# Mixture of experts in split fp32r: new order tables, a second matrix fetched in parts, and splits on GpSimd in two units

## The chip, the cores and the metric

The kernel runs on one core of a Trainium2 chip. The metric is the device time of one execution in microseconds (us). Engine names in the profile: PE is TensorE, PEld its weight loads, DVE is VectorE, ACT is ScalarE, POOL is GpSimd, SP is SyncE, which here only issues DMAs. A difference under about 0.5% is not told from none by a measurement of this kernel.

## The reference

```python
x = attention(...)                      # (2176, 512): windowed and 32 global tokens
h = np.maximum(x @ w_in, 0.0);  x = h * h @ w_out            # 512 -> 2048 -> 512
P = np.exp(x @ w_gate - max)            # 8 experts
for _ in range(8):                      # Sinkhorn
    P /= P.sum(1, keepdims=True) + 1e-09
    P /= P.sum(0, keepdims=True) + 1e-09
    P *= N / E
for e in range(E):                      # the second mixture, 512 -> 1024 -> 512
    out += P[:, e:e + 1] * (np.maximum(x @ w1[e], 0.0) @ w2[e])
```

Everything is fp32. The change concerns the last loop alone, which fills the program from about 584 us to its end.

## The kernel before, in words

Each fp32 operand is split into a high and a low fp32r part (hi = a cast by ScalarE, lo = operand minus hi, by VectorE or GpSimd), and a product is three matmuls: hi x hi, hi x lo, lo x hi. The second mixture goes over the 2176 tokens in three blocks of 5, 6 and 6 tiles of 128 (`TBS`). A *unit* is one block with one half of an expert's 1024 hidden columns; each block has 16 units (`NS`, `UE` = 2 for an expert). Each matrix product is done by a scheme with seven products in place of eight, on sums of quarter blocks: of the tokens (S1 to S4), of the first matrix and of the second (T1 to T4).

**Block 1** (`first_block`). For every unit s it runs `second_weights(s)` along with the hidden products (`second_hidden`, 14 of them, with a hook after each in which one more step of the other work is issued), then `second_out`, five output tiles of 12 matmuls (line 1121), each read out of PSUM by ScalarE's copy (line 1127, the first half of an expert) or VectorE's addition (line 1131). The output tiles rotate through three PSUM buffers, which the sums of the Sinkhorn iteration (line 851) use too, as that runs beside units 0 and 1. During the output tiles `first_weights(s + 1)` forms the next unit's first matrix: four sums by GpSimd (lines 980 to 986) into the tile `tw`, casts of them by ScalarE (line 997), lo parts by VectorE (line 1000); all forms are written to DRAM (`forms_kept`, line 1032) for blocks 2 and 3. `second_weights(s)` holds four GpSimd sums of the raw second matrix (lines 1010 to 1013), also into `tw`, and one DMA of 1 MB that keeps them in DRAM (`sums_kept`, line 1014); and, for four pieces of the raw matrix, hi by ScalarE (line 1019) and lo by VectorE (line 1021).

**Blocks 2 and 3**: 32 units, here numbered u = 0 to 31. Nothing is transformed again; forms and sums come back from DRAM. All engine work of a unit is listed in a table of `time:operation:arguments` (`USUAL`; `BEFORE_BLOCK` for u = 15, `AFTER_BLOCK` for u = 16); `plan` shifts each table to its unit's start and the operations of all units are issued in the order of these times. Only the order counts: an operation then starts when its engine reaches it and its semaphores allow it. The operations:
- `H:k`, k = 0 to 13: a hidden product, 6 matmuls of 128x384 (line 1373), 84 in a unit; `snap`, `add`, `relu` (lines 1378, 1382, 1386) read it out of PSUM.
- `sum`, `hi`, `lo` (lines 1346, 1333, 1337): the sums S1 to S4 of the hidden layer and the splits of all its quarters, in two halves each; `v` is VectorE, `g` GpSimd.
- `M:i:t`: output product i for tile t, 6 matmuls of 128x256 (line 1403), 126 in a unit, in the order of products 1, 2, 5, 6, 7, 4, 3. Product 5 needs S1, 6 needs S2, 7 needs S3, 4 needs A22, 3 needs S4. `out` gathers one into the accumulator, weighted by the gate (VectorE, line 1419).
- `whi:i`, `wlo:e:i` (lines 1307, 1311): the split of the second matrix for product i, by ScalarE, and by VectorE or GpSimd.
- A piece of the first matrix (256 KB, line 1272) is asked for by SP after each `H:k`, ten pieces ahead, in a ring of ten buffers: what is asked for after `H:0` to `H:3` is used by `H:10` to `H:13`.
- `sums` (line 1291) asks for the next unit's T1 to T4 (1 MB, into `tw`); `rows` (line 1284) for the raw rows of B11, B21 and B22 (two DMAs, 512 and 256 KB).

SP's DMAs are issued in order, and each waits also for the DMA eight before it, since eight semaphores go round.

Of the kernel before, what the change touches and what calls it, by code (L numbers as in the profile page):

```python
# [1596 lines left out]
```

## Time and profile before

| | us |
|---|---|
| median of 3 runs | 2036.81 |
| lowest and highest | 2036.24, 2044.15 |
| profiled execution, its own time | 2037.15 |
| its span, first to last instruction | 2035.3 |
| block 1, unit 0 begins | 584.06 |
| block 2, u = 0 begins (its `H:0`) | 1015.39 |
| u = 15 begins | 1485.71 |
| u = 16 begins | 1518.83 |
| u = 18 begins | 1587.64 |
| last unit, u = 31, begins | 1996.93 |

| engine | busy us, share of the span |
|---|---|
| PE | 1958.3 (96%) |
| DVE | 1500.4 (74%) |
| ACT | 1055.0 (52%) |
| POOL | 805.5 (40%) |

A row of the timeline is the start and length of an instruction (or of several alike in a row, x4), its engine, its line, the operation, output and input, and in brackets the idle time before it and what ended that. Busy time by stretch sums each engine's instructions in a piece of the span; PEclk is the granted TensorE clock as a share of the full one. The wait table sums an engine's idle time by the instruction that ended it.

### The profile page before, as it was taken

How to read it: one execution, taken by the hardware profiler on the slowest of the kernel's cores; microseconds unless marked ns; L12 is line 12 of the kernel's file. 1: busy time of each engine (PE TensorE's matmuls, PEld its weight loads, DVE VectorE, ACT ScalarE, POOL GpSimd, SP SyncE). 2: the span in 40 equal slices, each digit the busy share in tenths (PEclk: the TensorE clock that was granted, in tenths of full speed). 3: DMA queues.
4: the chain of work that ended last, by engine and by line, in shares of the span. 5: the costliest groups of instructions: out<-in, count | busy, mean ns of one | idle time of the engine just before them, and what ended most of it. 6: DMA issues, size and time to landing. Idle time of an engine off the chain costs nothing.

```text
span 2035.3 us, 34904 instructions
## 1 busy us (share of the span) xinstructions
PE 1958.3 (96%) x12482; PEld 1838.7 (90%) x12482; DVE 1500.4 (74%) x3013; ACT 1055.0 (52%) x2357; POOL 805.5 (40%) x815
## 2 busy tenths in 40 slices
PE   8998999999999999999999999999998999999998
PEld 6887798999888899999999999999988999999998
DVE  7999656666467877777777867778687786876867
ACT  7997442333244444444565555555555555555553
POOL 6546332223133455555333433434333342433433
PEclk8999999999999999999999999999999999999999
DMA  7675111112027777777764463553645445354461
GB/s 159 144 145 130 43 63 42 42 63 68 1 89 260 260 265 262 253 263 264 260 219 157 170 215 137 192 187 141 217 155 202 154 173 208 136 200 163 164 215 55
DMA packets 293229, 332.58 MB, mean 163 GB/s; under 512 B 106048, under 2 KB 210496, under 8 KB 286912
## 3 DMA queue, kind: packets, MB, share of 16 engines
q1 hardware_dynamic: 293056, 330.35, 49.5%
q8 instruction: 99, 1.62, 0.3%
q14 instruction: 74, 0.61, 0.1%
HBM read 239.88 MB, written 79.95 MB: 157 GB/s over the span
## 4 chain that ended last, share of the span: by engine, by line
PE 63%; DVE 16%; DMA 11%; ACT 7%; issue 1%; POOL 1%; SPq 1%; DVEq 0%; ACTq 0%; POOLq 0%
PE y L1121 11%; PE oy L1403 10%; DMA w<-forms_kept 10%; PE y L894 9%; PE h L254 9%; PE pa L1373 6%; PE pa L1058 5%; DVE xl L1337 3%; PE pm L1373 3%; DVE hf L1337 3%; DVE acc L1419 3%; DVE hs L1346 3%; PE pd L1058 2%; PE om L1403 2%; PE pb L1373 2%; ACT e L502 2%
## 5 line engine op out<-in xcount | busy, mean ns | idle before, releaser
L1373 PE MATMUL pa<-xh,w 128*128 128x384 f32 x1024 | 293.2, 337 | 16.6 <-DMA w<-forms_kept 15.0
L1373 PEld LDWEIGHTS pa<-xh,w 128*128 128x128 f32 x1024 | 187.8, 188 | 25.4 <-DVE xl L1337 19.1
L1337 POOL TENSOR_TENSOR xl<-acc,xh 128x384 fp32r<-128x384 f32 x64 | 65.4, 1021 | 356.6 <-ACT xh L1333 354.7
L1121 PE MATMUL y<-w,xh 128*128 128x512 f32 x640 | 200.0, 394 | 3.1 <-DVE w L1021 3.1
L894 PE MATMUL y<-hid,w 128*128 128x384 f32 (+1 forms) x960 | 191.1, 357 | 1.3 <-ACT rs L260 1.3
L894 PEld LDWEIGHTS y<-hid,w 128*128 128x128 f32 x960 | 171.8, 188 | 16.6 <-ACT rs L260 1.7
L254 PE MATMUL h<-xh,w 128*128 128x384 f32 (+1 forms) x640 | 181.9, 357 | 1.2 <-ACT rs L260 1.2
L1403 PE MATMUL oy<-w,hf 128*128 128x256 f32 x1152 | 151.6, 286 | 20.8 <-DVE hf L1337 16.6
L1373 PE MATMUL pa<-xl,w 128*128 128x384 f32 x512 | 171.3, 335 | 0.0
L1403 PEld LDWEIGHTS oy<-w,hf 128*128 128x128 f32 x1152 | 142.1, 191 | 27.4 <-DVE hf L1337 22.7
L1419 DVE SCALAR_TENSOR_TENSOR acc<-oy,prob,acc 128x256 f32<-128x256 f32 x366 | 163.6, 472 | 0.7 <-PE oy L1403 0.4
L1307 ACT CAST w<-tw 128x512 fp32r<-128x512 f32 x128 | 79.4, 620 | 162.2 <-PE oy L1403 140.1
L1346 POOL TENSOR_TENSOR hs<-acc 128x384 f32<-128x384 f32 x64 | 85.7, 1358 | 184.6 <-ACT acc L1386 184.6
L1373 PE MATMUL pm<-xh,w 128*128 128x384 f32 x512 | 150.4, 334 | 0.0
L1121 PEld LDWEIGHTS y<-w,xh 128*128 128x128 f32 x640 | 120.7, 190 | 27.9 <-DVE w L1021 3.5
L1403 PE MATMUL oy<-w,xh 128*128 128x256 f32 x768 | 140.7, 283 | 0.0
L260 ACT ACTIVATE r<-h 128x384 f32<-128x384 f32 (+1 forms) x76 | 40.4, 531 | 177.4 <-PE h L254 176.2
L1058 PE MATMUL pa<-xh,w 128*128 128x320 f32 x512 | 129.9, 311 | 0.9 <-DVE z L1074 0.9
L254 PEld LDWEIGHTS h<-xh,w 128*128 128x128 f32 x640 | 117.7, 188 | 14.3 <-ACT r L260 2.7
L115 POOL TENSOR_TENSOR cv<-cv,w 128x512 f32<-128x512 f32 x32 | 48.2, 1515 | 206.5 <-ACT w L113 131.7
L1382 DVE TENSOR_TENSOR acc<-pb,snaps 128x384 f32<-128x384 f32 x64 | 35.7, 557 | 127.3 <-PE pb L1373 124.7
L1121 PE MATMUL y<-w,xl 128*128 128x512 f32 x320 | 125.5, 392 | 0.0
(260 smaller groups left out, 5769.8 us busy)
## 6 DMA issues: line engine op xcount, KB each, us to landing
w<-forms_kept SPq DMA_DIRECT2D x448, 256.0 KB, 5.4
raw<-in_moe_w_dram SPq DMA_DIRECT2D x96, 512.0 KB, 4.9
forms_kept<-w SPq DMA_DIRECT2D x64, 512.0 KB, 6.3
tw<-sums_kept SPq DMA_DIRECT2D x32, 1024.0 KB, 7.5
forms_kept<-w SPq DMA_DIRECT2D x64, 384.0 KB, 6.0
sums_kept<-tw SPq DMA_DIRECT2D x16, 1024.0 KB, 7.6
raw<-in_moe_w_in_dram SPq DMA_DIRECT2D x16, 512.0 KB, 4.2
...
```

Of the source, the lines that this page charges most:

```text
L115: nc.gpsimd.tensor_tensor(out=top, in0=top, in1=f32(hi), op=ALU.subtract)
L254: nc.tensor.matmul(ps, lhsT=w, rhs=x, start=(k == 0), stop=(k == 3 * NC - 1))
L502: nc.scalar.activation(out=v, in_=v, func=AF.Exp, bias=st[:, c : c + 1], scale=-1.0, accum_out=st[:, 4 + c : 5 + c])
L894: nc.tensor.matmul(ps, lhsT=w, rhs=m, start=(f == 0 and x == 0), stop=(f == last and x == 2))
L1058: nc.tensor.matmul(ps, lhsT=lhs, rhs=rhs, start=(first and t == 0), stop=(t == 5), skip_group_check=True)
L1121: nc.tensor.matmul(ps, lhsT=lhs, rhs=rhs, start=(t == 0), stop=(t == 3 * UF - 1))
L1307: nc.scalar.copy(halves_of(out_form[i][0]), source_of(u, i))
L1337: engine.tensor_tensor(out=lo, in0=raws[name][:, q], in1=f32(hi), op=ALU.subtract)
L1346: engine.tensor_tensor(out=raws[name][:, q], in0=raws[a][:, q], in1=raws[b][:, q], op=op)
L1373: nc.tensor.matmul(ps, lhsT=lhs, rhs=rhs, start=(i in (1, 5, 2) and t == 0), stop=(t == 5), skip_group_check=True)
L1403: nc.tensor.matmul(ps, lhsT=lhs, rhs=rhs, start=(i in (5, 1, 2) and y == 0), stop=(y == 5), skip_group_check=True)
L1419: nc.vector.scalar_tensor_tensor(out=acc_, in0=ps, scalar=pr, in1=acc_, op0=ALU.mult, op1=ALU.add)
```

## The change

1. All tables of blocks 2 and 3 are new, and there is one more, `FIRST`, for u = 0. Each has a length of 29.71, where `AFTER_BLOCK` had 30.79.
2. `rows` and `sums` are gone. `raw:i` (`request_raw`) asks for the second matrix of one product, 256 KB, for the next unit; seven of these stand in each table, each behind the last reader of that buffer. The buffers are fixed.
3. In units 0 and 1 of block 1 (`gating`), GpSimd makes the four lo parts of the second matrix, and the four sums with their DMA (`keep_sums`) come after the fourth. In unit 0 the conversion starts with the first hook; before, four hooks went by first.

The lines of the changed kernel shift: 1010 to 1013 become 1012 to 1015, 1014 becomes 1017, 1019 becomes 1026, 1021 becomes 1029, 1127 becomes 1137, 1311 becomes 1313, 1337 becomes 1339, 1346 becomes 1348, 1419 becomes 1421.

```diff
-        add = nc.gpsimd.tensor_tensor
-        add(out=t1, in0=b12, in1=b11, op=ALU.subtract)
...
-        nc.sync.dma_start(out=sums_kept[s].rearrange("p i q d -> p (i q d)"), in_=t.rearrange("p i q d -> p (i q d)"))
+        def keep_sums():
+            add = nc.gpsimd.tensor_tensor
+            add(out=t1, in0=b12, in1=b11, op=ALU.subtract)
...
+            nc.sync.dma_start(out=sums_kept[s].rearrange("p i q d -> p (i q d)"), in_=t_)
+        gating = s < UE
+        if not gating:
+            keep_sums()
         yield
         for f in range(UF):
...
             nc.scalar.copy(hi, r[k][:, q])
             yield
-            nc.vector.tensor_tensor(out=lo, in0=r[k][:, q], in1=f32(hi), op=ALU.subtract)
+            engine = nc.gpsimd if gating else nc.vector
+            engine.tensor_tensor(out=lo, in0=r[k][:, q], in1=f32(hi), op=ALU.subtract)
             yield
             if f == UF - 1:
+                if gating:
+                    keep_sums()
                 for k in range(2):
                     load_pair_of_pieces(s + 1, k, 1)
...
             conv = second_weights(s)
-            wait = 4 if s == 0 else 0
-            hooks = itertools.count()
-            if not wait:
-                next(conv)
+            next(conv)
...
-                if next(hooks) >= wait:
-                    next(conv, None)
+                next(conv, None)
...
-    def request_rows(u):
-    def request_sums(u):
...
+    def request_raw(u, i):
         if u >= LAST:
             return
+        name = OUT_WEIGHT[i]
+        if name in SUMS_AT:
+            src = sums_kept[u % NS][:, SUMS_AT[name]]
+        else:
+            src = second_rows(u % NS, int(name[1]) - 1)[:, :, (int(name[2]) - 1) * DM // 2 :][:, :, 0 : DM // 2]
+        nc.sync.dma_start(out=raw_of(i), in_=src)
...
     USUAL = """
-        1.40:wlo:v:5 2.00:wlo:v:2 2.08:H:2 2.12:sums 2.23:snap:5:0 2.72:rows 3.13:H:3 3.28:add:A11:0
+        4.69:whi:3 4.95:wlo:v:6 5.07:raw:4 5.21:H:5 5.36:snap:5:1 5.55:wlo:v:3 5.73:whi:7 6.25:relu:A11:0
...
-    LENGTH = {USUAL: 29.71, BEFORE_BLOCK: 29.71, AFTER_BLOCK: 30.79}
+    LENGTH = {FIRST: 29.71, USUAL: 29.71, BEFORE_BLOCK: 29.71, AFTER_BLOCK: 29.71}
```

**VectorE in the output products of a usual unit.** `acc` with `hs` out of it is a quarter or a sum S of the hidden layer; `xl` and `hf` are lo parts (`hf` those of S2 and S3); `oy`, `ob`, `om`, `oa` are output products, gathered into `acc`. Before:

```order
L1337 TENSOR_TENSOR xl<-acc,xh 128x384
L1346 TENSOR_TENSOR hs<-acc 128x384
L1337 TENSOR_TENSOR xl<-hs,xh 128x384
L1419 SCALAR_TENSOR_TENSOR acc<-oy,prob,acc 128x256 x2
L1337 TENSOR_TENSOR xl<-hs,xh 128x384
L1346 TENSOR_TENSOR hs<-hs,acc 128x384 x2
L1419 SCALAR_TENSOR_TENSOR acc<-oy,prob,acc 128x256
L1419 SCALAR_TENSOR_TENSOR acc<-ob,prob,acc 128x256
L1337 TENSOR_TENSOR hf<-hs,hf 128x384 x4
L1419 SCALAR_TENSOR_TENSOR acc<-om,prob,acc 128x256
```

Now:

```order
L1339 TENSOR_TENSOR xl<-acc,xh 128x384
L1339 TENSOR_TENSOR xl<-hs,xh 128x384
L1348 TENSOR_TENSOR hs<-acc 128x384 x3
L1348 TENSOR_TENSOR hs<-hs,acc 128x384 x2
L1339 TENSOR_TENSOR xl<-hs,xh 128x384 x2
L1421 SCALAR_TENSOR_TENSOR acc<-oy,prob,acc 128x256 x2
L1421 SCALAR_TENSOR_TENSOR acc<-ob,prob,acc 128x256
L1348 TENSOR_TENSOR hs<-acc 128x384
L1339 TENSOR_TENSOR hf<-hs,hf 128x384 x2
L1421 SCALAR_TENSOR_TENSOR acc<-oy,prob,acc 128x256
L1421 SCALAR_TENSOR_TENSOR acc<-om,prob,acc 128x256
```

Five sums now stand together ahead of the first gathers, where splits and sums alternated before; VectorE makes two of the four lo parts of S2 and S3 instead of all four, and the other two have gone to GpSimd.

**GpSimd in the same unit.** Before:

```order
L1337 TENSOR_TENSOR xl<-acc,xh 128x384 x2
L1346 TENSOR_TENSOR hs<-acc 128x384 x2
L1346 TENSOR_TENSOR hs<-hs 128x384 x2
L1337 TENSOR_TENSOR xl<-hs,xh 128x384 x2
L1311 TENSOR_TENSOR w_71<-tw,w_71 128x512
L1311 TENSOR_TENSOR w_3120<-raw,w_3120 128x512
```

Now:

```order
L1339 TENSOR_TENSOR xl<-acc,xh 128x384 x2
L1339 TENSOR_TENSOR xl<-hs,xh 128x384
L1339 TENSOR_TENSOR hf<-hs,hf 128x384 x2
L1339 TENSOR_TENSOR xl<-acc,xh 128x384
L1348 TENSOR_TENSOR hs<-hs 128x384 x2
```

GpSimd no longer sums out of `acc` in this stretch; it splits instead, and its sums (S4, the last one used) are the only two left. The splits of the second matrix (line 1311) are gone from it.

**SP's queue in a usual unit.** `w` of `forms_kept` is a piece of the first matrix. Before, 1.75 MB stand in a row:

```order
L1272 DMA w_3564<-forms_kept 128x512
L1291 DMA tw<-sums_kept 128x2048
L1284 DMA raw<-in_moe_w_dram 128x2x512
L1284 DMA raw<-in_moe_w_dram 128x2x256
L1272 DMA w_3564<-forms_kept 128x512
L1272 DMA w_3565<-forms_kept 128x512 x2
L1272 DMA w_3566<-forms_kept 128x512 x2
```

Now:

```order
L1279 DMA w_3566<-forms_kept 128x512 x2
L1279 DMA w_3567<-forms_kept 128x512
L1300 DMA tw<-sums_kept 128x512
L1279 DMA w_3567<-forms_kept 128x512
L1279 DMA w_70<-forms_kept 128x512
L1300 DMA raw<-in_moe_w_dram 128x2x256
L1300 DMA tw<-sums_kept 128x512
L1279 DMA w_70<-forms_kept 128x512
L1279 DMA w_3564<-forms_kept 128x512
L1300 DMA tw<-sums_kept 128x512
L1279 DMA w_3564<-forms_kept 128x512
```

The requests for the second matrix now stand singly between the pieces, and further back.

**GpSimd in unit 0 of block 1.** Before:

```order
L986 TENSOR_TENSOR tw<-raw 128x256
L1010 TENSOR_TENSOR tw<-raw 128x512
L1011 TENSOR_TENSOR tw<-raw 128x512
L1012 TENSOR_TENSOR tw<-raw,tw 128x512
L1013 TENSOR_TENSOR tw<-raw,tw 128x512
L980 TENSOR_TENSOR tw<-raw 128x256
L982 TENSOR_TENSOR tw<-raw,tw 128x256
```

Now:

```order
L986 TENSOR_TENSOR tw<-raw 128x256
L1029 TENSOR_TENSOR w_71<-raw,w_71 128x512
L1029 TENSOR_TENSOR w_3394<-raw,w_3394 128x512
L1029 TENSOR_TENSOR w_3343<-raw,w_3121 128x512
L1029 TENSOR_TENSOR w_3343<-raw,w_3343 128x512
L1012 TENSOR_TENSOR tw<-raw 128x512
L1013 TENSOR_TENSOR tw<-raw 128x512
L1014 TENSOR_TENSOR tw<-raw,tw 128x512
L1015 TENSOR_TENSOR tw<-raw,tw 128x512
L980 TENSOR_TENSOR tw<-raw 128x256
L982 TENSOR_TENSOR tw<-raw,tw 128x256
```

The four splits stand ahead of the four sums, and the next unit's sums of line 980 behind both, as before.

## Rows read from the trace of the kernel before

**Rows 1.** Busy time by stretch, from unit start to unit start: us, each engine's busy time, PEclk
```profile
1015.39:1485.71 470.32, 454.98 (x3152) 445.55 (x3150) 354.94 (x692) 259.23 (x526) 178.44 (x152) 1.00 0.51 177
...
1518.83:1556.24 37.41, 31.99 (x212) 31.10 (x211) 31.28 (x58) 19.15 (x38) 11.36 (x10) 0.95 0.52 169
...
1996.93:2035.34 38.41, 30.66 (x212) 29.69 (x210) 24.73 (x46) 13.91 (x29) 9.45 (x8) 0.98 0.22 69
...
1587.64:1618.48 30.84, 30.30 (x213) 29.72 (x212) 23.55 (x47) 17.28 (x35) 11.81 (x10) 1.00 0.50 180
```

**Rows 2.** Chain of waits: start and length of a piece in us, what
```profile
664.71 13.62 PE y L1121 x60
...
1037.70 6.46 PE oy L1403 x52
...
1528.42 2.08 PE pa L1373 x12
```

**Rows 3.** Waits of TensorE, 1015.39 to the end: us in total, times, longest
```profile
PE oy L1403 <- DVE hf L1337: 16.6, 30, 1.3
PE pa L1373 <- DMA w<-forms_kept: 15.0, 22, 1.8
PE oy L1403 <- ACT hf L1333: 3.8, 1, 3.8
```

**Rows 4.** Timeline of VectorE, unit 18: start, us, instruction [idle before <-releaser]
```profile
1603.62 1.37 DVE L1337 TENSOR_TENSOR xl<-hs,xh 128x384 fp32r<-128x384 f32 x1
...
1605.70 0.58 DVE L1337 TENSOR_TENSOR xl<-hs,xh 128x384 fp32r<-128x384 f32 x1
...
1608.13 2.78 DVE L1337 TENSOR_TENSOR hf<-hs,hf 128x384 fp32r<-128x384 f32 x4
1610.83 0.47 DVE L1419 SCALAR_TENSOR_TENSOR acc<-om,prob,acc 128x256 f32<-128x256 f32 x1
```

**Rows 5.** Timeline of GpSimd, unit 18, same columns
```profile
1603.19 2.69 POOL L1346 TENSOR_TENSOR hs<-acc 128x384 f32<-128x384 f32 x2 [5.23 <-ACT acc L1386]
1606.91 2.18 POOL L1346 TENSOR_TENSOR hs<-hs 128x384 f32<-128x384 f32 x2 [1.03 <-DVE hs L1346]
1610.40 2.36 POOL L1337 TENSOR_TENSOR xl<-hs,xh 128x384 fp32r<-128x384 f32 x2 [1.31 <-ACT xh L1333]
...
1614.19 1.29 POOL L1311 TENSOR_TENSOR w<-raw,w 128x512 fp32r<-128x512 f32 x1
```

**Rows 6.** Timeline of SP's DMA queue, unit 18: start, us of issuing, DMA
```profile
1591.45 0.32 SPq L1291 DMA_DIRECT2D tw<-sums_kept  x1
```

**Rows 7.** Busy time by stretch, unit 18; the last three: PEclk, DMA share, GB/s
```profile
1592.00:1604.00 12.00, 12.00 (x74) 11.76 (x73) 6.05 (x12) 8.81 (x20) 2.84 (x3) 1.00 1.01 373
```

**Rows 8.** Busy time by stretch, units 0, 1 and a steady unit of block 1
```profile
584.06:620.16 36.10, 31.92 (x165) 26.31 (x164) 28.57 (x61) 15.88 (x34) 22.29 (x19) 0.95 0.64 211
620.16:650.66 30.50, 28.97 (x153) 25.78 (x152) 26.27 (x66) 12.06 (x27) 11.86 (x12) 0.94 0.64 217
...
678.17:704.11 25.94, 25.94 (x145) 23.58 (x144) 20.35 (x33) 11.48 (x26) 14.61 (x14) 1.00 0.77 261
```

**Rows 9.** Timeline of TensorE, unit 0 of block 1
```profile
606.80 0.50 PE L1121 MATMUL y<-w,xh 128*128 128x512 f32 x1 [3.12 <-DVE w L1021]
```

**Rows 10.** Busy time by stretch, unit 0 of block 1, after that wait
```profile
607.00:611.00 4.00, 4.00 (x11) 3.13 (x11) 4.00 (x6) 1.62 (x3) 3.22 (x5) 0.57 0.45 143
```

**Rows 11.** Timeline of GpSimd, unit 0 of block 1: sums, and line 980 behind them
```profile
587.78 1.73 POOL L1010 TENSOR_TENSOR tw<-raw 128x512 f32<-128x512 f32 x1
...
593.48 1.30 POOL L1013 TENSOR_TENSOR tw<-raw,tw 128x512 f32<-128x512 f32 x1
602.77 0.74 POOL L980 TENSOR_TENSOR tw<-raw 128x256 f32<-128x256 f32 x1 [7.98 <-DMA sums_kept<-tw]
```

**Rows 12.** Timeline of ScalarE, unit 0 of block 1
```profile
606.23 0.62 ACT L997 CAST w<-tw 128x512 fp32r<-128x512 f32 x1 [2.15 <-POOL tw L986]
607.68 0.59 ACT L1127 COPY acc<-y 128x512 f32<-128x512 f32 x1 [0.83 <-PE y L1121]
```

More of the change, by code (lines that the diff above doesn't have):

```diff
@@ L1229, in first_block @@
             else:
-                request_rows(0)
+                rawb.extend(stage.tile([P, 2, 512], F32, tag="r1", name="raw") for _ in range(2))
+                for i in OUT_ORDER:
+                    request_raw(0, i)
                 first_requests()
-                request_sums(0)
                 todo.append(form_splits(1))
@@ L1488 @@
-        32.59:tlo:v:S3 32.70:thi:S2 33.57:tlo:v:S2 34.91:tsum:v:S4 35.89:thi:S4 36.98:tlo:v:S4 37.85:out:4:1
-        38.71:out:4:2
+        -9.27:whi:2 -6.33:whi:6 -5.81:whi:5 -5.29:whi:1 -2.01:whi:4 -1.49:whi:7 -0.90:wlo:v:4 -0.30:wlo:g:7
+        0.00:H:0 0.15:whi:3 1.00:wlo:v:2 1.04:H:1 1.19:snap:1:0 1.60:wlo:g:3 1.72:raw:2 2.08:H:2 2.52:raw:7
+        3.13:H:3 3.28:add:A11:0 3.32:raw:4 3.75:wlo:v:5 4.17:H:4 4.32:thi:A11 4.35:wlo:v:6 4.47:raw:5
+        4.95:wlo:v:1 5.05:relu:A11:0 5.21:H:5 5.27:raw:6 5.47:snap:5:0 5.84:snap:5:1 5.94:tlo:v:A11
@@ new lines @@
+        6.07:raw:3 6.21:snap:1:1 6.25:H:6 6.58:hi:A11:0 6.87:raw:1 7.12:lo:g:A11:0 7.29:H:7 7.44:add:A11:1
+        7.44:thi:A12 8.17:snap:6:0 8.34:H:8 8.54:relu:A11:1 8.68:add:A12:0 9.15:tlo:v:A12 9.38:H:9
+        9.53:snap:6:1 9.90:relu:A12:0 10.32:hi:A11:1 10.42:H:10 10.57:add:A22:0 10.73:hi:A12:0
+        10.86:lo:g:A11:1 11.16:relu:A22:0 11.46:H:11 11.61:add:A12:1 11.86:lo:g:A12:0 12.20:relu:A12:1
+        12.50:H:12 12.65:add:A22:1 12.76:hi:A12:1 13.30:lo:v:A12:1 13.55:H:13 13.70:relu:A21:0
@@ L1490 @@
+        27.70:tsum:v:S3 28.27:M:3:1 28.57:tlo:v:S1 28.68:thi:S3 28.99:M:3:2 29.44:out:3:0 29.44:tsum:g:S2
+        29.83:out:4:0 30.22:out:3:2 30.61:out:3:1 31.00:out:2:1 31.39:tsum:v:S4 31.79:thi:S2 32.52:thi:S4
+        33.45:tlo:v:S2 34.32:tlo:v:S3 35.19:tlo:v:S4 37.73:out:4:1 44.24:out:4:2
     """
     AFTER_BLOCK = """
[L1492 to L1493 removed]
@@ L1499 @@
-        13.81:add:A22:1 13.90:hi:A12:1 14.40:relu:A22:1 14.44:lo:v:A12:1 14.62:H:13 14.82:relu:A21:0
-        14.91:wlo:v:2 15.20:hi:A22:1 15.51:sum:v:S1:0 15.63:rows 15.67:M:1:0 15.82:relu:A21:1
-        15.98:lo:v:A22:1 16.20:hi:S1:0 16.39:M:1:1 16.45:sum:v:S1:1 16.92:lo:v:S1:0 17.04:hi:S1:1 17.11:M:1:2
-        17.39:out:1:1 17.39:sum:g:S3:1 17.78:out:1:0 17.83:M:2:0 18.34:lo:v:S1:1 18.47:hi:S3:1 18.55:M:2:1
-        18.81:sum:v:S2:1 19.27:M:2:2 19.28:sum:v:S2:0 19.40:hi:S2:1 19.75:out:1:2 19.75:sum:g:S3:0
@@ new lines @@
+        9.73:wlo:v:3 9.90:relu:A12:0 10.33:wlo:v:2 10.42:H:10 10.46:hi:A12:0 10.87:relu:A11:1 10.93:add:A22:0
+        11.00:lo:g:A12:0 11.05:raw:2 11.43:hi:A11:1 11.46:H:11 11.61:add:A12:1 11.84:relu:A22:0 11.85:raw:1
+        12.26:relu:A12:1 12.50:H:12 12.65:raw:4 12.65:add:A22:1 12.82:hi:A12:1 13.12:lo:v:A11:0 13.45:raw:6
+        13.55:H:13 13.59:lo:v:A11:1 13.70:relu:A21:0 14.06:lo:v:A12:1 14.08:relu:A22:1 14.25:raw:3
+        14.53:sum:g:S1:0 14.59:M:1:0 14.74:relu:A21:1 15.05:raw:7 15.31:M:1:1 15.46:out:1:0 15.85:sum:v:S1:1
@@ new lines @@
+        15.85:raw:5 16.03:M:1:2 16.32:sum:v:S2:0 16.43:hi:S1:1 16.75:M:2:0 16.79:sum:v:S3:1 16.84:hi:S1:0
+        17.25:hi:S2:0 17.26:sum:v:S2:1 17.47:M:2:1 17.73:lo:v:S1:0 17.84:hi:S2:1 18.19:M:2:2 18.20:lo:v:S1:1
+        18.25:hi:S3:1 18.67:out:1:2 18.67:sum:g:S4:0 18.91:M:5:0 19.06:out:1:1 19.45:out:2:2 19.60:hi:A22:0
+        19.63:M:5:1 19.84:lo:v:S2:0 20.01:hi:S4:0 20.31:lo:v:S2:1 20.35:M:5:2 20.78:sum:v:S3:0 21.07:M:6:0
+        21.25:lo:v:S3:1 21.36:hi:S3:0 21.77:hi:A22:1 21.79:M:6:1 21.90:lo:g:S3:0 21.94:out:6:0 22.33:out:5:0
@@ L1535, in plan @@
                 "sum": left_sum,
-                "whi": lambda i: weight_hi(u, i),
-                "wlo": lambda e, i: weight_lo(e, u, i),
-                "rows": lambda: request_rows(u + 1),
-                "sums": lambda: request_sums(u + 1),
+                "whi": weight_hi,
+                "wlo": weight_lo,
+                "raw": lambda i: request_raw(u + 1, i),
                 "out": unit.gather,
```

150 lines of the change are left out of this document (74 added, 76 removed).

## The prediction

> **What bounds the kernel now.** I first cut the span at the starts of the units of blocks 2 and 3 (busy time by stretch) to see which engine is full and what each unit costs [rows 1]: 31 units, from 1015.39 to 1996.93, take 981.54 us, 31.66 each, and TensorE is busy for all but about 1 us of each, at clock 1.00 (0.95 in unit 16). The chain of waits then gives the price of undisturbed products [rows 2]: 12 matmuls of a hidden product 2.08 us, so 84 cost 14.56; 52 of an output product 6.46, 0.124 each with the end of the last, about 0.121 without, so 126 cost 15.2. The floor of a unit is therefore 29.8 us, and a unit loses 1.9 on the average. Which waits these are is read from TensorE's waits in that stretch [rows 3]: 30 waits for the lo form of S2 (VectorE, line 1337) at M:6, 22 for a piece of the first matrix at the last hidden products, and one of 3.8 us for ScalarE, in unit 16.
>
> The first kind: VectorE's timeline of unit 18 shows a split of 128x384 at 0.58 us undisturbed but at 1.37 at 1603.62, and four at 2.78 from 1608.13, two of them slow [rows 4]. GpSimd's timeline shows what ran beside them: sums that start at 1603.19 and at 1606.91 [rows 5]. The gathers, which read PSUM, stay at 0.47 beside GpSimd's work of 1610.40. Two operations lose 0.8 each; 1.1 of it reaches TensorE. Unit 18 has only this loss: 30.84 less 1.1 is 29.7, which confirms the floor. So the shown idle time (16.6 over 30) is about half of the loss, the rest being the refill behind it.
>
> The second kind: SP asks for 1 MB of sums and 0.75 MB of rows in one go, from 1591.45 on [rows 6], with the pieces for H:10 to H:13 queued behind them; the queues move 373 GB/s over those 12 us, all they can [rows 7]. 15.0 us in 22 units are shown; the remainder 1.9 - 1.1 makes it 0.6 to 0.8 a unit.
>
> The first block is bound by TensorE too, but units 0 and 1 take 36.10 and 30.50 [rows 8], where a steady unit is 25.94: a wait of 3.12 for the fourth lo split [rows 9] and 4 us at clock 0.57, the lower level (1.2 of 2.4 GHz), after that idle time [rows 10], a loss of 0.43 x 4 = 1.7.
>
> **Part 1: tables and requests in seven parts.** They move together. What each removes:
> - VectorE now does S1 and S3 before M:1's gathers, and GpSimd's sum of S3 is gone; GpSimd has only splits there. Its split of S2's second half follows VectorE's last operation with two SBUF inputs in that stretch and lies beside gathers. Adding the row durations (0.47 a sum, 0.58 a split, 0.39 a gather, 1.1 a GpSimd split) from unit start, S2 is complete at about 20.5 and M:6 begins at 21.07; S3 has 1.3 in hand, S4 0.6, A22 over 2. Price of the wait: 1.1 to 0. I take 0, with 0.2 us in hand (see rival 2).
> - SP now asks for the pieces of H:10 to H:13 ahead of the first raw part (due 5.07), and each 256 KB part stands alone among the pieces. The second wait goes, 0.7 to 0. The last part, raw:2, is asked for at about 11.6 and needed by ScalarE's whi:2 at 20.4, 9 us later; parts of this size move in under 1 us each at 373 GB/s, with up to four pieces in front. Four more DMAs a unit (21 for 17) cost SP some 0.3 us each of issue [rows 6], and SP has slack; each also waits for the DMA eight before it. I take 0.
> - Unit 16's 3.8 us [rows 3]: ScalarE's cast of unit 17's rows comes late because the old table asks at 15.63; the new one asks at 11.05 and the stall goes. Unit 15 keeps some of its 33.12 (1485.71 to 1518.83): token forms add VectorE work; I leave +1 for the two.
>
> A rule of the Trainium skill speaks against the seven parts ("DMA: Bandwidth & Descriptors", section "Measured (HBM→SBUF, 128 partitions, SWDGE, issued from GpSimd)"): DMAs are to be batched to 1 MiB, and its fit for one is 2.0 us plus bytes/436e3. By it 21 of 256 KB in series would be 2.6 each, 55 us, and each unit would be DMA-bound: an estimate from that page alone. The trace speaks otherwise, since pieces of that size, several in flight, move at 373 GB/s [rows 7].
>
> Sum of units 0 to 30: 31 x 29.8 + 1 = 924.8 against 981.54: **-56.7**. The last unit, 38.41, loses the same two waits: **-1.7** (its tail of gathers and output DMAs stays).
>
> **Part 2: the first two units of block 1.** Added on GpSimd: four lo splits of 128x512. It does such a split in 1.29 at 1614.19 [rows 5], and its sums of that size vary from 1.30 to 1.73 [rows 11]; I take 1.3 and keep 1.7 for the range. VectorE gives up four. The conversion in unit 0 starts at once, and ScalarE's casts fall at about 5.6, 7.8, 9.3 and 12.3 into the unit, so the fourth lo ends near 14.2, ahead of the first out product at 17.2: the 3.12 goes.
>
> What is queued behind: the four sums and their 1 MB DMA now stand after the fourth lo, and all later work on `tw` waits for that DMA. The four sums, the first at 1.73 and the last at 1.30 [rows 11], take 6.0 together, to 20.2. GpSimd's next weight sum (line 980) waited 7.98 for that DMA before [rows 11]: to 28.2. Its four take 602.77 to 606.2, 3.4: to 31.6. ScalarE's cast of them (line 997, 0.62) stands ahead of the copy of the first out tile (line 1127, 0.59) in its order [rows 12]: the copy ends at 32.8. Before, the cast ended at 606.85 and hid in the wait. The third out tile needs that tile's buffer (three, one held by the Sinkhorn product). It is due at 22.8: 10 of 12 matmuls were done when TensorE stopped at 603.68, then 0.45 and one tile of 13.62/5 = 2.72 [rows 2, 9]. So TensorE waits 10 us, then does three tiles, 8.2, with 1.7 of slow clock: the unit ends at 42.7 against 36.10, **+6.6**. Unit 1 goes the same way: fourth lo at 9.6, sums to 15.6, DMA to 23.8, sums to 27.4, casts and splits, the add of tile 1 on VectorE, so the fourth tile starts at about 30, where 25.94 - 5.45 = 20.5 would be due; plus 5.45 and 1.7 is 37.2 against 30.50, **+6.7**. From unit 2 on nothing changes. Bounds: the waits may not bite at all (rival 1), or the lo splits take 1.7 and the DMA is slower beside the pieces, +2 a unit more: -7 to +17. I take the order as it stands: **+13.3**.
>
> **Sum**: -56.7 - 1.7 + 13.3 = -45.1. The profiled execution took 2037.15 us (span 2035.3), 0.34 over the median of 2036.81; 2037.15 - 45.1 = 1992.0, against the median 1991.7: **1992 us**.
>
> **Rivals.**
> 1. *The move to GpSimd brings what it takes away.* If the sums' DMA comes back sooner, or the copy isn't held by the cast, units 0 and 1 lose the 3.12 and 1.7, and unit 1 about 2.5: -7 in place of +13: **1971 us**. For it: DMA traffic is light in those microseconds. Against: the 7.98 in rows 11 had an idle queue too. 0.12.
> 2. *The collision stays.* GpSimd's split of S2 gets in ahead of VectorE's last split; the margin is 0.2 us. Then a VectorE operation takes 1.37 for 0.58 and M:6 waits 0.8 in each of 31 units: +25, **2017 us**. For it: rows 4, where it happened in every unit. Against: GpSimd's input (ScalarE's cast) comes after VectorE has begun. The Trainium skill ("SBUF — State Buffer", section "Who interferes with whom") says that whichever of the two issues first holds the shared ports for its whole instruction; by that, 0.2 us decides all of it, and rows 4 agree. 0.13.
> 3. *The parts don't relieve the pieces.* The change does not do what it says: the total per unit is still 5.5 MB (180 GB/s over 30.84 us in unit 18 [rows 1]), and H:13 waits 0.6 as before: +19, **2010 us**. Against: they need 15 of 29.8 us at the rate of rows 7. 0.08.
> 4. *Slower: the last part lands too late.* ScalarE works in order; if raw:2, the last of a unit's 21 DMAs, is not there at whi:2, all behind it waits, hi of S4 first, and M:3 is late. The slack ends about 25.7 after unit start (27.55 less cast, sum and split). That is 14 us after the request; it takes a mean rate below some 210 GB/s over the unit. Each microsecond beyond costs 31: 3 us give +93, **2085 us**; past 1.5 us it is slower than before. Against: 373 GB/s [rows 7]. 0.04.
>
> **How the numbers follow.** Forecast 0.63, rivals 0.12, 0.13, 0.08 and 0.04. Of the forecast's own case the bounds of part 2 (-2 to +4) and of the residual loss a unit (0.0 to 0.3: 9 us) give 1984 to 2005. The range takes in rivals 1 to 3: **1969 to 2017**; outside lie rival 4 and the ends. A difference of 0.5%, 10 us, is about what a measurement of this kernel tells from none. All cases but rival 4 are faster by more; two rivals together would end at 2036, so same 0.03, slower 0.04, faster 0.93.
>
> **What would show it.** Right: units of 29.7 to 29.9 us between starts of H:0; no wait of TensorE for hf (lo of S2) at M:6 or for a piece at H:13; VectorE's splits at 0.58; unit 16 like the others; in block 1 a wait of about 10 us of the third out tile for the copy behind ScalarE's cast of `tw`, and GpSimd's line 980 waiting for the sums' DMA. Wrong: splits at 1.37 beside GpSimd (rival 2), pieces late (3), ScalarE idle at whi for DMA (4), or units 0 and 1 of block 1 at 31 and 28 us (1).

## The result and the profile after

The changed kernel takes **1979.33 us** (median of 4 runs, 1978.40 to 1979.49), the kernel before 2038.06 (4 runs); the ratio is 0.9706, 95% interval 0.9685 to 0.9727. The forecast was 1992 with a range of 1969 to 2017, so the time lies inside, 13 us under the forecast. The profiled execution's span is 1976.6 against 2035.3, 58.7 less. By unit starts that is:

| stretch | before | after | difference | forecast |
|---|---|---|---|---|
| units 0 to 30 of blocks 2 and 3 | 981.54 | 919.32 | -62.2 | -56.7 |
| last unit, to the end | 38.41 | 36.25 | -2.2 | -1.7 |
| all ahead of u = 0 (block 1) | 1015.39 | 1021.03 | +5.6 | +13.3 |

Busy time by stretch of the changed kernel, answering to [rows 1]: units 0 to 14, unit 9, unit 16, and the last.

```profile
1021.03:1466.17 445.14, 444.77 (x3151) 444.56 (x3150) 345.18 (x714) 254.50 (x529) 126.69 (x123) 1.00 0.57 187
1288.37:1318.01 29.64, 29.64 (x213) 29.64 (x212) 23.07 (x48) 16.90 (x35) 8.16 (x8) 1.00 0.58 187
1495.82:1525.45 29.63, 29.63 (x212) 29.63 (x211) 27.32 (x56) 17.49 (x37) 8.99 (x8) 1.00 0.66 218
1940.35:1976.60 36.25, 29.79 (x212) 29.59 (x210) 24.52 (x52) 16.28 (x34) 8.16 (x8) 0.94 0.24 73
```

All units but the first (30.27) and the last (36.25, with the end of the program) take 29.63 to 29.67, and in unit 9 TensorE is busy for its whole 29.64 us. Unit 16, 37.41 before, is like the others. In TensorE's waits from u = 0 to the end, the three rows of [rows 3] are gone; this one row is all that is left:

```profile
PE oy L1405 <- DVE acc L1421: 0.4, 1, 0.4
```

VectorE's and GpSimd's timelines of unit 9 (start, us, instruction), answering to [rows 4, 5]:

```profile
1305.07 1.02 DVE L1339 TENSOR_TENSOR xl<-hs,xh 128x384 fp32r<-128x384 f32 x2
...
1308.31 1.02 DVE L1339 TENSOR_TENSOR hf<-hs,hf 128x384 fp32r<-128x384 f32 x2
```

```profile
1305.85 1.12 POOL L1339 TENSOR_TENSOR hf<-hs,hf 128x384 fp32r<-128x384 f32 x1 [5.36 <-ACT hf L1335]
1309.09 1.12 POOL L1339 TENSOR_TENSOR hf<-hs,hf 128x384 fp32r<-128x384 f32 x1 [2.12 <-ACT hf L1335]
...
1311.14 2.00 POOL L1348 TENSOR_TENSOR hs<-hs 128x384 f32<-128x384 f32 x2
```

VectorE's pairs of splits take 1.02, 0.51 each; from u = 0 on two splits of 1.36 and 1.37 are left (both in unit 0, which has its own table), where 62 of about 1.4 stood. GpSimd's split at 1305.85 starts 0.24 us before VectorE's last is done (1305.07 + 1.02) and takes 1.12 for the 1.02 of an undisturbed one: here GpSimd waits a little, not VectorE.

Block 1, units 0 and 1, answering to [rows 8]: busy time by stretch; then TensorE's timeline of unit 0 with the two waits that matter, and GpSimd's and ScalarE's [rows 9, 11, 12].

```profile
583.79:622.97 39.18, 32.62 (x165) 26.38 (x164) 26.49 (x57) 15.73 (x34) 21.04 (x19) 0.96 0.60 194
622.97:655.85 32.88, 29.25 (x153) 26.13 (x152) 27.30 (x60) 12.33 (x27) 20.82 (x18) 0.95 0.56 187
```

```profile
601.59 0.41 PE L1068 MATMUL pa<-xh,w 128*128 128x320 f32 x1 [1.13 <-DVE z L1084]
...
613.09 0.79 PE L1131 MATMUL y<-w,xh 128*128 128x512 f32 x2 [3.79 <-ACT acc L1137]
```

```profile
596.69 1.30 POOL L1029 TENSOR_TENSOR w<-raw,w 128x512 fp32r<-128x512 f32 x1 [1.64 <-ACT w L1026]
...
602.35 1.43 POOL L1015 TENSOR_TENSOR tw<-raw,tw 128x512 f32<-128x512 f32 x1
608.89 0.73 POOL L980 TENSOR_TENSOR tw<-raw 128x256 f32<-128x256 f32 x1 [5.11 <-DMA sums_kept<-tw]
```

```profile
611.94 0.62 ACT L997 CAST w<-tw 128x512 fp32r<-128x512 f32 x1 [6.95 <-POOL tw L986]
612.46 0.58 ACT L1137 COPY acc<-y 128x512 f32<-128x512 f32 x1
```

The wait of 3.12 for the fourth lo split is gone, and one of 3.79 stands in its place: the third output tile waits for ScalarE's copy of the first, which stands behind the cast of `tw`, which waits for line 980's sums, which wait for the DMA of the second matrix's sums.

### The profile page after: what moved, and what is told of

Same layout as the page of the kernel before. It is cut to its first block, busy times and chain, and to the rows that moved or that the text cites. A ratio compares the mean times of both kernels' runs of the same rounds, so it can differ in the third digit from the quotient of the medians.

```text
span 1976.6 us, 35103 instructions
## 1 busy us (share of the span) xinstructions
PE 1934.5 (98%) x12482; PEld 1835.3 (93%) x12482; DVE 1477.4 (75%) x3063; ACT 1041.3 (53%) x2357; POOL 711.5 (36%) x765
## 4 chain that ended last, share of the span: by engine, by line
PE 87%; DVE 4%; ACT 3%; DMA 2%; POOL 2%; SPq 1%; issue 1%; DVEq 0%; POOLq 0%; ACTq 0%
PE oy L1405 14%; PE pa L1375 13%; PE y L1131 10%; PE y L894 9%; PE h L254 9%; PE pm L1375 7%; PE pa L1068 5%; PE om L1405 5%; PE ob L1405 3%; PE pb L1375 3%; PE pd L1068 2%; PE oa L1405 2%; PE pb L1068 1%; ACT e L502 1%; SPq L288 1%
## 5 line engine op out<-in xcount | busy, mean ns | idle before, releaser
L1375 PE MATMUL pa<-xh,w 128*128 128x384 f32 x1024 | 285.8, 334 | 0.0
L1339 POOL TENSOR_TENSOR xl<-acc,xh 128x384 fp32r<-128x384 f32 x96 | 96.9, 1024 | 416.9 <-ACT xh L1335 416.9
L1421 DVE SCALAR_TENSOR_TENSOR acc<-oy,prob,acc 128x256 f32<-128x256 f32 x366 | 172.1, 478 | 21.7 <-PE oy L1405 19.0
L894 PEld LDWEIGHTS y<-hid,w 128*128 128x128 f32 x960 | 171.9, 188 | 16.6 <-ACT rs L260 1.7
L1380 ACT COPY snaps<-pa 128x384 f32<-128x384 f32 x128 | 61.4, 479 | 185.2 <-PE pa L1375 181.0
L1339 POOL TENSOR_TENSOR hf<-hs,hf 128x384 fp32r<-128x384 f32 x63 | 71.2, 1131 | 230.6 <-ACT hf L1335 230.6
L1335 ACT CAST xh<-hs 128x384 fp32r<-128x384 f32 x192 | 95.4, 512 | 99.7 <-POOL hs L1348 83.4
L1405 PE MATMUL oy<-w,hf 128*128 128x256 f32 x1152 | 142.2, 282 | 0.0
```

The costliest lines, as they stand in the source:

```text
L894: nc.tensor.matmul(ps, lhsT=w, rhs=m, start=(f == 0 and x == 0), stop=(f == last and x == 2))
L1335: nc.scalar.copy(part_of(hidden_form(name), 0, q), raws[name][:, q])
L1339: engine.tensor_tensor(out=lo, in0=raws[name][:, q], in1=f32(hi), op=ALU.subtract)
L1375: nc.tensor.matmul(ps, lhsT=lhs, rhs=rhs, start=(i in (1, 5, 2) and t == 0), stop=(t == 5), skip_group_check=True)
L1380: nc.scalar.copy(snaps[:, at, 0:n], src[q])
L1405: nc.tensor.matmul(ps, lhsT=lhs, rhs=rhs, start=(i in (5, 1, 2) and y == 0), stop=(y == 5), skip_group_check=True)
```

## The experiments

Each kernel ran with the kernel before beside it on the same chip; ratios are to that. Between parts of the table the ratios are to be compared, not the times.

| kernel | us | ratio to before, 95% interval | a usual unit of blocks 2, 3 |
|---|---|---|---|
| before | 2038 | | 31.4 |
| changed | 1979.33 | 0.9706 (0.9685 to 0.9727) | 29.63 |
| block 1 as before | 1970.60 | 0.9669 (0.9641 to 0.9697) | 29.63 |
| sums first | 1969.11 | 0.9653 (0.9630 to 0.9676) | 29.63 |
| copy first | 1975.18 | 0.9684 (0.9661 to 0.9707) | 29.63 |
| sums first and copy first | 1969.89 | 0.9658 (0.9631 to 0.9685) | 29.63 |
| S3, S4 pushed back on VectorE | 2092.78 | 1.0243 (1.0211 to 1.0276) | 31.9 to 34.3 |
| requests later | 2021.19 | 0.9896 (0.9866 to 0.9926) | 30.83 |
| S3, S4 pushed back and requests later | 2065.05 | 1.0108 (1.0081 to 1.0134) | 31.9 to 33.8 |
| one request, late | 1982.59 | 0.9706 (0.9686 to 0.9725) | 29.63 |
| order of the output phase | 2028.41 | 0.9936 (0.9907 to 0.9965) | 30.3 to 32.7 |
| that and requests later | 2002.20 | 0.9814 (0.9775 to 0.9854) | 30.23 |
| S3 on GpSimd, ahead of a relu | 2040.80 | 0.9998 (0.9983 to 1.0012) | 31.77 |
| S3 on GpSimd | 2015.05 | 0.9880 (0.9855 to 0.9904) | 30.87 |

My theory had three separate causes. VectorE is slowed by GpSimd at M:6; the pieces of H:10 to H:13 queue behind the second matrix; block 1's part costs time since the sums' DMA is late. Rivals: block 1's part pays; the small size of the seven parts is what helps; VectorE's amount of work, not the collision, sets M:6.

### Block 1

**Block 1 as before**, on the changed kernel:

```diff
-        gating = s < UE
+        gating = False
...
+            wait = 4 if s == 0 else 0
...
-                next(conv, None)
+                if next(hooks) >= wait:
+                    next(conv, None)
```

> The changed kernel with units 0 and 1 of block 1 as before (lo splits on VectorE, sums first, four hooks of delay in unit 0); tables and seven parts stay. Theory: the block 1 part of the change costs 5.6 us (units 0 to 2 take 39.2, 32.9 and 28.0 where 36.1, 30.5 and 27.5 stood), so u = 0 begins again at about 1015.4 and the time is about 1973.7. Rival: that part relieves something else (the pieces for u = 0, or the Sinkhorn work beside it), and the time is 1979 or more.

1970.60 us. u = 0 begins at 1012.79 where the changed kernel has 1021.03, so the block 1 part of the change costs 8.2 us and the rival falls (the ratios' intervals overlap a little; the unit starts show it). That is 2.6 more than the two kernels' first traces give, and the reason is in this run's row of unit 1:

```profile
583.57:619.82 36.25, 31.91 (x165) 26.28 (x164) 28.18 (x61) 15.88 (x34) 22.04 (x19) 0.95 0.61 208
619.82:648.30 28.48, 27.36 (x153) 24.50 (x152) 25.15 (x65) 11.96 (x27) 10.91 (x12) 1.00 0.64 216
```

Its code is that of the kernel before, but the unit takes 28.48 and not 30.50 and the clock stays at 1.00: its wait for the Sinkhorn steps was 1.1 us where it was 1.5, and no stretch at the lower level followed. Of the 2.6 us that stretch is 1.7 and the shorter wait 0.4; unit 2 has most of the rest. So the price of the block 1 part is 5.6 or 8.2 us, and the difference is mostly whether the old code meets that stretch in the execution compared.

**Sums first**, on the changed kernel:

```diff
-        if not gating:
-            keep_sums()
+        keep_sums()
...
-                if gating:
-                    keep_sums()
```

> The changed kernel with the four sums and their DMA of units 0 and 1 of block 1 first on GpSimd, and the lo splits, still by GpSimd, behind them. Theory (what is late is line 980 behind the sums' DMA, because the sums stand behind the fourth lo): the sums end at about 594.8, line 980 starts at 603 and not 609, and the fourth lo is there at about 600, before the first output product at 601; no wait of 3.8 and no stretch of slow clock: unit 0 about 32, unit 1 about 28.5, time about 1967. Rival (GpSimd splits are too slow there: they run beside VectorE's two-input work and delay the hidden products, whatever their order): units 0 and 1 stay at 36 and 31 or more, time 1975 or more.

1969.11 us, 10.2 under the changed kernel: **the lowest median of all kernels here, ahead of both given ones**. The ratios tell it apart from the changed kernel (0.9630 to 0.9676 against 0.9685 to 0.9727). They do not tell it apart from block 1 as before, 1.5 us above, nor from the run with both edits below. Busy time by stretch, and GpSimd's timeline of unit 0:

```profile
583.31:616.35 33.04, 30.85 (x164) 25.16 (x164) 28.37 (x57) 15.72 (x34) 25.13 (x21) 1.00 0.60 204
616.35:645.53 29.18, 27.69 (x153) 24.51 (x152) 25.10 (x60) 12.00 (x27) 17.85 (x18) 1.00 0.66 235
```

```profile
592.73 1.29 POOL L1015 TENSOR_TENSOR tw<-raw,tw 128x512 f32<-128x512 f32 x1
593.98 5.34 POOL L1028 TENSOR_TENSOR w<-raw,w 128x512 fp32r<-128x512 f32 x4
601.66 1.01 POOL L980 TENSOR_TENSOR tw<-raw 128x256 f32<-128x256 f32 x1 [2.34 <-DMA sums_kept<-tw]
```

The sums end at 594.0, the four lo splits at 599.3 (5.34 for four, 1.34 each), and line 980 starts at 601.66. Both waits are gone and the clock is 1.00 in both units. The splits on GpSimd cost nothing here; what costs is that the sums stand behind them. Whether they gain anything over block 1 as before is not shown by the times: units 0 and 1 take 62.2 together where they took 64.7 there.

**Copy first**, on the changed kernel: the hook behind an output tile of units 0 and 1 is called after the tile is read out.

```diff
-            hook()
+            early = tb == 0 and u < UE
+            if not early:
+                hook()
             s, pr = acc_t[:, j, d], prob[:, j, e : e + 1]
...
+            if early:
+                hook()
```

> The changed kernel, with an output tile of units 0 and 1 of block 1 read out of PSUM before the steps of the next unit's weights are issued, so that ScalarE's copy no longer stands behind its cast of tw. Theory (the third tile waits for the copy behind the cast): the 3.8 us wait at 613.09 and the slow clock behind it go; the forms of unit 1 end at about 620, just when its hidden products begin; unit 0 about 34.5, unit 1 about 31, time about 1973. Rival (the forms of the next unit are what is late, the copy is not the limit): the wait moves to the first hidden products of unit 1, unit 0 and the wait behind it together unchanged, time 1978 to 1980.

1975.18 us, between theory and rival. The ratios do not tell it from the changed kernel, but the traces do: unit 0 took 34.96 for 39.18, and u = 0 begins at 1017.10 for 1021.03. TensorE's wait in unit 0 (timeline) is still for a copy of ScalarE:

```profile
613.38 0.74 PE L1131 MATMUL y<-w,xh 128*128 128x512 f32 x2 [1.13 <-ACT acc L1139]
```

It is now the copy of the second tile that stands behind the cast, one tile (2.72 us) later, and of the 3.79 there is 1.13 left. So the order on ScalarE is the place, and line 980's lateness the cause; the rival's wait at unit 1's first products didn't come.

**Both**, sums first and copy first:

> The changed kernel with both edits: the sums of units 0 and 1 of block 1 first, and the tiles read out ahead of the next unit's steps. Theory: what the first leaves (the cast of tw at about 606.2 ahead of the copy of tile 0, under 1 us a unit) goes too, units 0 and 1 about 31 and 28, time about 1966. Rival: the reading out isn't the limit once the sums are first, and it equals the run with the sums first alone within 1 us.

1969.89 us against 1969.11: nothing more, as the rival said. With the sums first, the copy was no limit.

### The requests

**Requests later**, on the kernel before:

```diff
-        1.40:wlo:v:5 2.00:wlo:v:2 2.08:H:2 2.12:sums 2.23:snap:5:0 2.72:rows 3.13:H:3 3.28:add:A11:0
+        1.40:wlo:v:5 2.00:wlo:v:2 2.08:H:2 3.14:sums 2.23:snap:5:0 3.15:rows 3.13:H:3 3.28:add:A11:0
```

> The kernel before, with the request for sums and rows in the usual table moved from 2.12 and 2.72 to 3.14 and 3.15, so behind the piece asked for after H:3; size and number of the DMAs unchanged. Theory (the pieces of H:10 to H:13 are late because they are queued behind 1.75 MB, 0.6 to 0.7 us a unit): no wait of TensorE for a piece at H:10 to H:13, units about 30.8, time about 18 us under before, some 2019. Rival (the total traffic of the first half of a unit is what makes pieces late, or the seven small parts are needed): the wait stays or moves to the whi, and the time is within 8 us of before.

2021.19 us, 1.0% under before. TensorE's waits from u = 0 on:

```profile
PE oy L1403 <- DVE hf L1337: 16.6, 30, 1.3
...
PE pa L1373 <- DMA w<-forms_kept: 1.0, 1, 1.0
```

22 waits for a piece are down to one, and the usual units, 30.8 to 32.7 before (31.4 on the average), are 30.83 nearly all: two numbers in a table, 0.6 us a unit. The waits for hf have not changed by a tenth, 16.6 in 30.

**One request, late**, on the changed kernel: at the seventh `raw` of a table, the whole second matrix in three DMAs (1 MB, 512 and 256 KB).

```diff
+        asked[u] = asked.get(u, 0) + 1
+        if asked[u] < len(OUT_ORDER):
+            return
...
+        nc.sync.dma_start(out=t, in_=sums_kept[u % NS].rearrange("p i q d -> p (i q d)"))
+        nc.sync.dma_start(out=rawb[1][:, :, 0:DM], in_=second_rows(u % NS, 1))
+        nc.sync.dma_start(out=rawb[0][:, :, 0 : DM // 2], in_=second_rows(u % NS, 0)[:, :, 0 : DM // 2])
+        return
```

> The changed kernel with the second matrix of a unit asked for in one go (1 MB, 512 and 256 KB as before) at the place where the last of the seven parts stood; tables unchanged. Theory (the order against the pieces of H:10 to H:13 counts, not the size of the parts): units stay at 29.6 to 29.8, time within 5 us of 1979. Rival (the seven parts are what frees the pieces): the next pieces wait behind 1.75 MB, or whi:2 waits for the rows, 0.5 us or more a unit, time 1995 or more.

1982.59 us. Units stay at 29.63, with one of 33.75: unit 16, whose table has its last `raw` at 15.85, so that unit 17's matrix comes too late. The last unit is 1.2 us longer too. So the parts as such bring nothing in the usual units; what counts is that they are asked for behind H:3. That they are separate matters in unit 16 alone, where the first part can be asked for at 11.05.

### VectorE and GpSimd

**S3 and S4 pushed back on VectorE**, on the kernel before (ScalarE's casts of S3 go back with their sums):

```diff
-        16.21:sum:g:S3:1 ... 18.57:sum:g:S3:0 ... 21.40:sum:g:S4:1 ... 22.35:sum:g:S4:0
+        20.00:sum:v:S3:1 ... 20.02:sum:v:S3:0 ... 21.41:sum:v:S4:1 ... 22.34:sum:v:S4:0
```

> The kernel before, with the sums of S3 in the usual table (30 units) moved from GpSimd to VectorE behind its last lo of S2, and those of S4 to VectorE as well, so that no GpSimd operation runs beside VectorE's sums and splits of S1 to S3. Requests as before. Theory (two VectorE operations lose 0.8 us each beside GpSimd, of which 1.1 reaches M:6): no wait for lo of S2 at M:6, units 30.3 instead of 31.4, time about 33 us under before, some 2004. Rival (M:6 waits for VectorE's amount of work and not for the collision): two to four sums more on VectorE move the wait to M:7 or M:3, and the time is within 10 us of before.

2092.78 us, 2.4% slower: a miss. The waits from u = 0 on:

```profile
PE oy L1403 <- DVE acc L1419: 29.2, 30, 1.0
PE oy L1403 <- ACT xh L1333: 18.0, 29, 0.6
PE pa L1373 <- DMA w<-forms_kept: 10.9, 18, 1.2
```

The wait for hf is gone as it should be, and two others stand in its place, for a gather (VectorE) and for hi of S4, about 1 and 0.6 us in each unit. About half of the loss is not these waits but TensorE's clock: from u = 0 on it was at 0.50 in 15 stretches, 14 of them behind such a pair of waits, and 27 us went there. The kernel before has one such stretch, a loss of 1.7 us (the end of the program aside in both). Taking the work from GpSimd is not enough; VectorE's order has to make room for it. **Both edits** together, expected at 1987:

> The kernel before with both edits (sums of S3 and S4 on VectorE, requests behind the piece of H:3). Theory (two separate waits at different places of a unit): the gains add, units near the floor at 29.7 to 29.9, about 50 us under before, some 1987; what then remains against the changed kernel is unit 16 (3.8 us at most with u = 15) and block 1's 5 to 8 us the other way. Rival (one wait covers the other): the sum is well short of the two single gains.

2065.05: the requests' gain adds (28 us between the two kernels), the loss stays. Of its 28 usual units 17 take 31.9 and 11 take 33.4 to 33.8; all have the same two waits, and in those 11 the clock fell behind them. The run says nothing of the collision's price.

**Order of the output phase**, on the kernel before: in `USUAL`, all `sum` and `out`, and `hi` and `lo` of S1 to S4 and of A22's second half, take the changed kernel's times; the rest stays.

> The kernel before with, in the usual table alone (30 units), the order of the output phase taken from the changed kernel: all sums, the splits of S1 to S4 and of A22's second half, and the gathers. Requests, splits of the second matrix and everything else as before. Theory (the loss at M:6 is the collision of GpSimd's sums of S3 with VectorE, and the new order removes it without a new wait, unlike the run in which the sums were simply pushed to the back of VectorE): no wait for lo of S2 at M:6, the DMA waits stay, units about 30.3 where 31.4 stood, about 33 us under before. Rival (the new order works only with the second matrix's splits moved into the hidden phase too, since VectorE would be too full in the output phase): a wait for a gather or for S4 appears, and the time is within 15 us of before or above.

2028.41 us, 0.6% under before, some 13 us: the rival's side. The waits for hf are gone and the DMA's stay (18.8 us in 23), as the theory has it, but a short one has come for lo of S4:

```profile
PE om L1403 <- DVE xl L1337: 6.2, 29, 0.2
```

**That and requests later**:

> The same, and sums and rows asked for behind the piece of H:3 (3.14 and 3.15). Theory: both waits gone, units 29.6 to 29.9, about 50 us under before; the seven parts and the moved splits are then worth nothing of their own except in unit 16. Rival: as for the run before, units of 30.5 or more.

2002.20 us, units 30.23: half of the 1.2 between 30.83 and 29.63 is gained, half not. VectorE's and GpSimd's timelines of its unit 9, and TensorE's at M:3, the last product:

```profile
1310.71 2.11 DVE L1337 TENSOR_TENSOR xl<-hs,xh 128x384 fp32r<-128x384 f32 x2
```

```profile
1309.54 1.29 POOL L1311 TENSOR_TENSOR w<-tw,w 128x512 fp32r<-128x512 f32 x1
1310.79 1.62 POOL L1311 TENSOR_TENSOR w<-raw,w 128x512 fp32r<-128x512 f32 x1
```

```profile
1312.88 0.39 PE L1403 MATMUL om<-w,xl 128*128 128x256 f32 x1 [0.21 <-DVE xl L1337]
```

VectorE's two splits of S4 take 2.11, not 1.02, since GpSimd's splits of the second matrix (line 1311) run beside them; M:3 waits 0.21 by the profile, and the product takes 0.46 more than in the changed kernel (2.62 for 2.16 us); the other 0.14 of the unit's 0.60 is in the hidden products. The kernel before has GpSimd split S4 there, one after the other with line 1311, so this wait is new: the collision of M:6 at another place. The changed kernel makes the second matrix's splits on VectorE, six of seven in the hidden phase, and takes 29.63. The new order of the output phase needs that; the theory's "29.6 to 29.9" missed it. The rival named the place, though for another reason, that VectorE would be too full. No run moves these splits alone; that line 1311 is the cause is read from the rows.

**S3 on GpSimd, ahead of a relu**, on the changed kernel: `sum:v:S3:0` and `sum:v:S3:1` given to GpSimd at 14.68 and 14.69.

> The changed kernel with the two sums of S3 in the usual table given back to GpSimd at the place of the first (14.68). Theory (a VectorE operation with two SBUF inputs that starts while GpSimd runs takes 1.37 instead of 0.56): GpSimd's two sums run from about 1302.6 to 1305.3 in the unit from 1288.37, two of VectorE's sums or splits beside them show 1.37, VectorE has 0.7 more to do than now, which is about its slack at M:6: units 29.7 to 30.2, time 1982 to 1997. Rival (the duration at 1603.62 had another cause): all of VectorE's splits stay at 0.5 to 0.6, and units at 29.63.

2040.80 us and 31.77 a unit. The second sum reads here a half of A21 that its relu has not passed, and the relu waits for the sum, so VectorE stands idle for 2.4 us ahead of S1. Two effects are mixed, and nothing follows on the price. The same with the second sum at 15.20, **S3 on GpSimd**:

> The changed kernel with the two sums of S3 in the usual table given back to GpSimd, at 14.68 and, now behind the relu of A21 that the second one reads, at 15.20; nothing else. (In the run before this the second sum stood ahead of that relu, so it summed a half that the relu had not yet passed, and held the relu up; its 31.77 a unit mixes that with what was asked.) Theory (a VectorE operation with two SBUF inputs that starts while GpSimd runs takes 1.3 to 1.4 for 0.56): GpSimd runs sums from about 14.5 to 17 after unit start and its two hf splits behind them, two to four of VectorE's sums and splits show 1.3 to 1.4, and M:6 or M:5 waits again: units 29.9 to 31.0, time 1988 to 2021. Rival (without the old order of the rest, there is slack enough): collisions show in VectorE's rows, but units stay at 29.63.

2015.05 us; units are 30.87, 1.24 over the changed kernel, in all 29 units with that table and in no other. VectorE's timeline of its unit 9, GpSimd's, and TensorE's wait at M:6's third tile:

```profile
1316.62 1.83 DVE L1348 TENSOR_TENSOR hs<-hs,acc 128x384 f32<-128x384 f32 x2
1318.37 1.01 DVE L1339 TENSOR_TENSOR xl<-hs,xh 128x384 fp32r<-128x384 f32 x2
...
1320.49 2.55 DVE L1339 TENSOR_TENSOR hf<-hs,hf 128x384 fp32r<-128x384 f32 x2
```

```profile
1314.89 2.68 POOL L1348 TENSOR_TENSOR hs<-acc 128x384 f32<-128x384 f32 x2 [2.18 <-ACT acc L1388]
1319.08 2.26 POOL L1339 TENSOR_TENSOR hf<-hs,hf 128x384 fp32r<-128x384 f32 x2 [1.51 <-ACT hf L1335]
```

```profile
1323.49 0.73 PE L1405 MATMUL oy<-w,hf 128*128 128x256 f32 x4 [0.94 <-DVE acc L1421]
```

GpSimd's sums run from 1314.89 to 1317.57, and VectorE's pair at 1316.62 takes 1.83; the pair at 1318.37, with GpSimd idle, 1.01; the pair at 1320.49, which starts behind GpSimd's of 1319.08, 2.55. With two sums less to do VectorE is later by 1.5 us, and its gather holds up M:6, which takes 3.39 us where it takes 2.16 in the changed kernel. That settles the collision. The rival that VectorE's amount of work sets M:6 falls too: the program is the same but for two sums moved from VectorE to GpSimd, and they cost 1.24 us a unit.

## Why the prediction held, point by point

- **The floor.** 29.8 was forecast, 29.63 measured, in every unit from the second to the last but one (29.67 at most). The output matmuls were rounded up: (29.63 - 14.56)/126 is 0.1196 each, not 0.121. That is 5 of the 13 us by which the forecast is too high; block 1, below, is most of the rest.
- **The range.** The forecast's own case was 1984 to 2005, and its two bounds, -2 and 0 off 1992, give 1990 as the lower end, not 1984. The measured 1979 lies below either. The time is inside the range of 1969 to 2017 because that takes in rival 1, which did not happen. Floor and block 1 were both put too high, so by the forecast's own terms it is luck that the range holds it.
- **Units 15 and 16.** The +1 left for them was not needed: 29.65 and 29.63.
- **The wait at M:6** went, and its price was right: 1.1 in [rows 3, 4], 1.20 by the units (30.83 with the requests moved, 29.63 now), 1.24 when GpSimd's two sums are put back. What I did not say is that GpSimd's two splits of the second matrix had to go too: with them about 0.5 of it comes back at M:3.
- **Rival 2, the collision stays**, was kept out by a small margin. GpSimd's split does not follow VectorE's last one, as I had it, but starts 0.24 us before that is done, and it is GpSimd that is stretched. The Trainium skill ("SBUF — State Buffer", section "Who interferes with whom") says: "Issue order, not op shape, decides who blocks." Rows of both kinds agree on who loses (1.12 on GpSimd here, 2.55 for VectorE's pair above). GpSimd lost 0.10 here, though, and not the whole 0.24 that were left of VectorE's split. The gathers, one operand in PSUM, stay at 0.47 to 0.49.
- **The wait at H:13** went, for the reason given, the order behind H:3. The rule of the Trainium skill weighed against the seven parts ("DMA: Bandwidth & Descriptors", section "Measured (HBM→SBUF, 128 partitions, SWDGE, issued from GpSimd)") did not decide: 21 DMAs a unit, all of 256 KB, and 17, two of them larger, gave the same 29.63. No run here has them issued by GpSimd, as that section's were.
- **Rival 4, the last part too late**, was nearer than I worked out. SP's and ScalarE's timelines of unit 9:

```profile
1302.79 0.38 SPq L1300 DMA_DIRECT2D raw<-in_moe_w_dram  x1
```

```profile
1309.70 0.62 ACT L1309 CAST w<-raw 128x512 fp32r<-128x512 f32 x1 [0.76 <-DMA raw<-in_moe_w_dram]
```

raw:2 is asked for 14.4 us into the unit, not 11.6, as each DMA waits for the one eight before it, which I had taken as 0, and lands at 21.3, where ScalarE already waits 0.76 for it. Of the 14 us between 11.6 and the point at 25.7 from which it decides, 9.7 were used up; 4.4 are left.
- **Block 1: the mechanism right, the term mis-sized**, +13.3 for +5.6 by the first traces, +8.2 against the run with block 1 as before. Every link of unit 0 shows: fourth lo done at 597.99, 14.2 into the unit as forecast; sums to 603.8; line 980 behind the DMA; cast; copy; third tile. Three steps were off. (1) "GpSimd's next weight sum waited 7.98 for that DMA before", taken as the DMA's own time, and in rival 1 as one with "an idle queue": before, it stood behind four DMAs of forms, 1.8 MB (first row below, from the kernel before: 379 GB/s); now it waits 5.11. (2) The third tile was due 25.5 into the unit and not 22.8, since the hidden products were late too: VectorE's step of line 1078 takes 1.17 for 0.48 beside the moved sums (second row), and TensorE waits 1.13 at 601.59 and 0.52 at 605.78. So the wait was 3.79 and not 10. (3) In unit 1 "25.94 - 5.45 = 20.5 would be due" came from a unit without the Sinkhorn work. The fourth tile was due at 26.7 and waited 0.63, not 9.5; most of the 2.4 us lost there is the wait for VectorE's Sinkhorn steps (last rows, before and changed), which GpSimd's sums slow down as well (636.35: 1.01 for 0.30). The stretch of slow clock behind it, 1.7, is in both kernels.

```profile
595.00:599.00 4.00, 4.00 (x29) 4.00 (x29) 3.90 (x12) 2.18 (x5) 0.00 (x0) 1.00 1.05 379
```

```profile
599.97 1.17 DVE L1078 SCALAR_TENSOR_TENSOR xl<-z,xh 128x320 fp32r<-128x320 f32 x1
```

```profile
PE m L851 <- DVE prob L846: 1.5, 1, 1.5
...
PE m L851 <- DVE prob L846: 3.0, 2, 2.1
```

- **Rival 1** gave 1971 for a block 1 part that pays. The run with the sums first ends near that, at 1969.11, but not by rival 1's sum: its units 0 and 1 gain 4.4 us on those of the kernel before (62.2 for 66.6), not 7, and the lower floor of the units gives the rest. What made the part cost in the changed kernel was the place of the sums.
